# Attention ahead of two dense layers on one core: U of two heads on the two column halves of TensorE, row sums by a product of their own, scores as fp32 products

## The chip, the cores and the metric

One core of a Trainium2 chip runs the whole program. The metric is the device time of one execution in microseconds (us); of the kernel before there are three timed executions, and their median is the number that counts. One further execution was recorded by the hardware profiler, and every duration below comes from that one. The engines are named PE (TensorE, with PEld for its weight loads), DVE (VectorE), ACT (ScalarE), POOL (GpSimd) and SP (SyncE, which issues the transfers).

## The reference, cut to what matters

Attention over 2 batches of 12 heads, 448 positions, 64 values a head, causal; then a dense layer of 768 to 1024 with a softmax gate and a layer norm, back to 768; then a second dense layer 768 to 2048 to 768. Only the attention is touched by the change.

```python
scores = scale * np.matmul(q, k.transpose(0, 1, 3, 2))
mask = np.triu(np.ones((seq, seq), dtype=bool), k=1)
scores = np.where(mask, -1000000000.0, scores)
scores = scores - np.max(scores, axis=-1, keepdims=True)
attn = np.exp(scores)
attn = attn / (np.sum(attn, axis=-1, keepdims=True) + 1e-09)
return np.matmul(attn, v).astype(np.float32)
...
h = x @ w_in
...
return (ln @ w_out).astype(np.float32)
...
h = np.maximum(x @ w_in, 0.0)
return (h * h @ w_out).astype(np.float32)
```

## The kernel before

The 24 heads are worked as 12 pairs. Of a pair, head 0 lies on SBUF partitions 0 to 63 and head 1 on 64 to 127, so a score product of one head uses one half of the array's rows. Two number formats occur on PE: F32R, a rounded fp32, which the dense layers and the scores use, and plain fp32, which U uses. To keep the scores exact in F32R, k and q are split in a high part (`kq_hi`, op H, L242, on ACT, tile HI) and a low rest (`kq_lo`, op L, L246, on DVE, tile LO), and `scores` (ops Sa and Sb, L317) adds three products: HI·HI, LO·HI and HI·LO.

For each pair, in order: the raw maxima of the scores are taken from HI alone (`max_mm`, ops S0a to S0c, L257, tile mxp; `max_red`, L272, on DVE), turned by PE (mT, L284) and brought to the other layout by a transfer (row, rowd; tile MR). Sa and Sb then compute the scores with the keys on the partitions, in two halves of 512 columns: Sa holds the blocks of 448 and 64 columns, Sb those of 320 and 192 (table `HALF`), and a last product with MR subtracts the maxima (L325; for pair 0 by L333). ACT takes the exponential of a half (ops ea1 and eb1, L349, tile PP, 5 buffers), POOL clears what lies above the diagonal (ka, kb, L346). `pv` (ops Ua and Ub, L358) multiplies by V in plain fp32: the tile VR holds for each head 64 columns of V and 64 columns of ones, so that the product U has the 64 outputs of a head on partitions 0 to 63 and the row sums on 64 to 127, head by head, each in a PSUM bank of its own. ACT copies U to E (L369), and transfers carry the sums to a small tile, their reciprocals to DRAM, and from there as `bc` back over the partitions; POOL multiplies (norm, L399, once for each head), and ACT and DVE split the result in two parts, the tiles xT (L407, L411).

What follows is `h_tile` (L474, products h of the first dense layer), its softmax and norm, `y0` and `y1` (L621), and the second dense layer (L756, products h and o).

The order of all this up to y1 is written out by hand: the string `SEQ` lists operations as name.index, and each engine executes its own in that order. PSUM is four slots of two banks, handed out in the order of SEQ (`bank2`, `give`). SP issues the transfers in the same order. The split weights w of the dense layers are made by DVE, ACT and, in the second layer, POOL.

## Time and profile before

| | us |
|---|---|
| median of 3 executions | 458.17 (457.73 to 458.36) |
| the profiled execution, whole | 457.37 |
| its span from first to last instruction | 455.6 |
| PE busy | 448.8 (99%) |
| DVE, ACT, POOL busy | 274.8, 164.2, 121.8 |

A page of the profile has the busy time of each engine, the span in 40 slices, the chain of work that ended last (followed back from the last instruction to what released each step), and groups of equal instructions. Further views list groups with each tile shape apart, one stretch in order of time, or the busy time of all engines in chosen stretches. A busy share near 100% of one engine together with a chain that lies almost wholly on it means that the sum of that engine's work sets the time. In these views a plain fp32 matmul appears as two records, an F32R one as one; a shape such as 64\*128 ahead of a tile's size is rows times columns of the array that a matmul uses.

### The profile page before, as it was taken

The numbers are of one execution on the slowest core, as the hardware profiler recorded it, in microseconds if no ns is written. First come the engines' busy times: TensorE is split into PE (matmuls) and PEld (weight loads), VectorE is DVE, ScalarE is ACT, GpSimd is POOL, SyncE is SP. The second block draws the span as 40 slices with busy tenths as digits, with TensorE's granted clock in tenths as the row PEclk, the third lists the DMA queues.
The fourth block names the chain that finished last, engine by engine and source line by source line (L and its number), as shares of the span: only waits on it lengthen the run. The fifth ranks groups of instructions, "written<-read, shape, count | busy, mean of one in ns | idle before, by whom it ended". The sixth has DMA issues, their size and how long they took to land.

```text
span 455.6 us, 6327 instructions
## 1 busy us (share of the span) xinstructions
PE 448.8 (99%) x2439; PEld 392.7 (86%) x2439; DVE 274.8 (60%) x524; ACT 164.2 (36%) x211; POOL 121.8 (27%) x122
## 2 busy tenths in 40 slices
PE   8999999999999999999999999999999999999996
PEld 6777777787888899988899999999999999999995
DVE  8889787756669998741347566665763424343221
ACT  3465665523556626231133333424331011210101
POOL 3125546364321011110021322313223131132310
PEclk9999999999999999999999999999999999999999
DMA  8357766232172360000042423424343342733403
GB/s 253 129 156 222 223 169 160 57 93 75 41 293 123 109 238 2 0 1 0 0 139 70 140 84 124 126 83 138 74 134 98 111 135 74 241 104 124 120 19 121
DMA packets 41400, 52.45 MB, mean 115 GB/s; under 512 B 18202, under 2 KB 32026, under 8 KB 40986
## 3 DMA queue, kind: packets, MB, share of 16 engines
q1 hardware_dynamic: 41370, 52.05, 37.1%
q8 instruction: 19, 0.31, 0.3%
q14 instruction: 11, 0.09, 0.1%
HBM read 49.16 MB, written 2.80 MB: 114 GB/s over the span
## 4 chain that ended last, share of the span: by engine, by line
PE 96%; DVE 0%; ACT 0%; issue 0%
PE h L756 25%; PE o L756 25%; PE h L474 13%; PE y L621 13%; PE U L358 10%; PE s L317 5%; PE mxp L257 2%; PE s L325 1%; PE T L599 1%; PE mxp L284 0%; PE s L333 0%; DVE o L790 0%; ACT o L790 0%
## 5 line engine op out<-in xcount | busy, mean ns | idle before, releaser
L756 PE MATMUL h<-yT,w 128*128 128x480 f32 x576 | 115.4, 362 | 0.0
L756 PE MATMUL o<-g,w 128*128 128x480 f32 x576 | 115.4, 362 | 0.0
L756 PEld LDWEIGHTS h<-yT,w 128*128 128x128 f32 x576 | 107.9, 187 | 7.4
L756 PEld LDWEIGHTS o<-g,w 128*128 128x128 f32 x576 | 107.9, 187 | 7.3
L677 POOL TENSOR_TENSOR w<-wf,w 128x768 fp32r<-128x768 f32 x32 | 59.3, 1852 | 203.0 <-ACT w L674 203.0
L674 ACT CAST w<-wf 128x768 fp32r<-128x768 f32 x32 | 26.8, 836 | 134.8 <-DVE wf L151 103.5
L149 DVE TENSOR_SCALAR wf<-raw 128x768 int32<-128x768 int32 (+1 forms) x46 | 26.8, 582 | 79.6 <-DMA raw<-in_moe_w_out_dram 51.7
L474 PE MATMUL h<-w,xT 128*128 128x512 f32 x252 | 59.5, 393 | 0.0
L621 PE MATMUL y<-lnT,w 128*128 128x384 f32 (+1 forms) x288 | 58.5, 363 | 0.0
L621 PEld LDWEIGHTS y<-lnT,w 128*128 128x128 f32 x288 | 51.9, 188 | 5.6
L474 PEld LDWEIGHTS h<-w,xT 128*128 128x128 f32 x252 | 46.8, 188 | 9.6
L358 PE MATMUL U<-PP,VR 128*128 128x448 f32 (+1 forms) x192 | 49.2, 400 | 0.3
L150 DVE SCALAR_TENSOR_TENSOR wf<-raw,wf 128x768 int32<-128x768 int32 (+1 forms) x46 | 47.2, 1027 | 1.6
L151 DVE SCALAR_TENSOR_TENSOR wf<-raw,wf 128x768 int32<-128x768 int32 (+1 forms) x46 | 46.5, 1011 | 1.6
L358 PEld LDWEIGHTS U<-PP,VR 128*128 128x128 f32 x192 | 32.1, 190 | 16.6 <-issue 11.4
L399 POOL TENSOR_TENSOR x<-E,bc 64x448 f32<-64x448 f32 x24 | 32.2, 1341 | 45.9 <-DMA bc<-d 42.9
L272 DVE CUSTOM_DVE_ANT_0 JK<-mxp,MK 112x336 bf16<-112x336 f32 (+2 forms) x96 | 38.8, 445 | 9.4 <-PE mxp L257 8.5
L349 ACT ACTIVATE PP<-s 128x1024 f32<-128x1024 f32 x24 | 24.5, 1023 | 12.9 <-PE s L325 7.2
L738 DVE TENSOR_TENSOR relu<-h,relu 128x896 f32<-128x896 f32 x16 | 17.5, 1092 | 14.6 <-ACT relu L737 14.6
L346 POOL TENSOR_SCALAR_AFFINE_SELECT PP<-PP 128x256 f32<-128x256 f32 (+1 forms) x48 | 20.5, 459 | 20.1 <-ACT PP L349 19.5
L740 ACT CAST g<-relu 128x896 fp32r<-128x896 f32 x16 | 15.1, 942 | 18.6 <-DVE relu L738 18.6
L650 DVE TENSOR_TENSOR yT<-y,yT 128x384 fp32r<-128x384 f32 (+1 forms) x12 | 7.4, 624 | 22.4 <-ACT yT L649 22.4
(75 smaller groups left out, 348.2 us busy)
## 6 DMA issues: line engine op xcount, KB each, us to landing
raw<-in_moe_w_out_dram SPq DMA_DIRECT2D x24, 768.0 KB
raw<-in_moe_w_in_dram SPq DMA_DIRECT2D x16, 768.0 KB
r<-in_kq_dram SPq DMA_DIRECT2D x12, 448.0 KB
VR<-in_v_dram SPq DMA_DIRECT2D x12, 256.0 KB
raw<-in_moe_w_in_dram SPq DMA_DIRECT2D x12, 256.0 KB
raw<-in_moe_w_in_dram SPq DMA_DIRECT2D x3, 1024.0 KB
bc<-d SPq DMA_DIRECT2D x12, 224.0 KB
out_dram<-o SPq DMA_DIRECT2D x6, 240.0 KB
```

The costliest lines, as they stand in the source:

```text
L149: nc.vector.tensor_scalar(xi, hw, 3, 0x3FFFFFFF, ALU.logical_shift_left, ALU.bitwise_and)
L150: nc.vector.scalar_tensor_tensor(xi, hw, -0x40000000, xi, ALU.bitwise_and, ALU.bitwise_or)
L151: nc.vector.scalar_tensor_tensor(xi, lw, 29, xi, ALU.logical_shift_right, ALU.bitwise_or)
L272: nc.vector.tensor_tensor_reduce(JK[t], b[0:JP, h, o : o + nk], MK[:, S - nk :], 1.0, NEG, ALU.add, ALU.max, mx[i][:, 4 * h + t : 4 * h + ...
L349: nc.scalar.activation(PP[n % NPP], sb[n], AF.Exp, scale=0.125)
L358: nc.tensor.matmul(UB[i][:, h, q0:S], VR[i % 3][:, t, h, :], PP[(2 * i + a) % NPP][:, h, o : o + nq], start=t == 0, stop=t == 2,)
L399: nc.gpsimd.tensor_tensor(x[D * h : D * h + D], e[0:D, h], bc[:, h], ALU.mult)
L474: nc.tensor.matmul(b[:, half, :], xT[c][s][:, t * P : t * P + P], W1[c][:, w, 512 * half : 512 * half + 512], start=(c == 0 and s == 0 and ...
L621: nc.tensor.matmul(b[:, ci, 0:n], WO[fi][:, w, c * P : c * P + P], M["lnT"][a][s][:, fi, :], start=(fi == 0 and w == 0 and s == 0), stop=( ...
L674: nc.scalar.copy(W2[n][:, 0], w_f["2", n])
L677: nc.gpsimd.tensor_tensor(W2[n][:, 1], w_f["2", n], f(W2[n][:, 0]), ALU.subtract)
L756: nc.tensor.matmul(flat(b)[:, o : o + n], w[:, wp, c : c + P], ops[s][:, x : x + n], start=first and r == 0, stop=last and r == 2,)
```

## The change

`pv` gives head 0 the columns 0 to 63 of the array and head 1 the columns 64 to 127: V of a head is 64 columns without ones, both heads write one PSUM bank, on different partitions, and the loops are turned so that the heads alternate. The row sums come from two new operations: `row_add` (op ad) adds on POOL the blocks of a pair's two halves that belong to the same query positions, with three additions into a new tile `ps`; `row_sum` (op Us) multiplies PP and `ps` with a tile of ones, again one head on each half of the columns, 448 columns a head. `scores` makes one plain fp32 product straight from k and q in place of the three of F32R; kq_lo, LO and the raw tiles are gone, k and q land in four buffers KQ, and H reads them. `u_out` becomes two ACT instructions, the sums leave by two transfers and `bc` comes back by two, norm is one instruction over both heads. PP has 6 buffers. SEQ is a new order of everything up to y1.

```diff
-KLO_POOL = (0,)
-NPP = 5
+NPP = 6
+NKQ = 4
...
 SEQ = """
-load_r.0 fl.0 fl.1 fl.2 fl.3 H.0 load_r.1 fl.4 L.0 S0b.0 S0c.0 mxb.0 fl.5 S0a.0 fl.6 mxc.0 fl.7 mxa.0 H.1 load_r.2
...
+fl.0 fl.1 fl.2 load_r.0 fl.3 H.0 fl.4 load_r.1 fl.5 H.1 S0c.0 load_r.2 S0a.0 S0b.0 fl.6 fl.7 lq.0 load_r.3 lq.1 mxc.0
...
             def load_r(i):
-
-                kq_raw[i] = t = raw.tile([P, 2, S], F32, tag="r", name="r")
-                nc.sync.dma_start(t, kq[i])
+                nc.sync.dma_start(KQ[i % NKQ][:, :, 0:S], kq[i])
...
             def scores(n):
                 i, a = divmod(n, 2)
-                HIk, HIq, LOk, LOq = (x[i % 3][:, j] for x in (HI, LO) for j in range(2))
+                K, Q = (KQ[i % NKQ][:, j] for j in range(2))
                 s = sb[n] = bank2("s")
-                first = True
-                for K, Q in ((HIk, HIq), (LOk, HIq), (HIk, LOq)):
-                    for t, o, q0, nq in HALF[a]:
-                        for h in range(2):
-                            r = slice(D * h, D * h + D)
-                            nc.tensor.matmul(
-                                s[:, h, o : o + nq], K[r, P * t : P * t + P], Q[r, q0 : q0 + nq], start=first, stop=False
-                            )
-                        first = False
+                for t, o, q0, nq in HALF[a]:
+                    for h in range(2):
+                        r = slice(D * h, D * h + D)
+                        nc.tensor.matmul(
+                            s[:, h, o : o + nq],
+                            K[r, P * t : P * t + P],
+                            Q[r, q0 : q0 + nq],
+                            start=t == HALF[a][0][0],
+                            stop=False,
+                        )
...
-                for h in range(2):
-                    for t, o, q0, nq in HALF[a]:
+                for t, o, q0, nq in HALF[a]:
+                    for h in range(2):
                         nc.tensor.matmul(
-                            UB[i][:, h, q0:S],
+                            UB[i][D * h : D * h + D, 0, q0:S],
                             VR[i % 3][:, t, h, :],
                             PP[(2 * i + a) % NPP][:, h, o : o + nq],
...
+            def row_add(i):
+
+                pa, pb = (PP[(2 * i + a) % NPP] for a in range(2))
+                ps[i] = p = lat.tile([P, 2, Q2], F32, tag="ps", name="ps", bufs=2)
+                nc.gpsimd.tensor_tensor(p, pa[:, :, 512 - Q2 :], pb[:, :, 512 - Q2 :], ALU.add)
+                for o, x in ((P, pb[:, :, 0 : Q2 - P]), (2 * P, pa[:, :, 0 : Q2 - 2 * P])):
+                    nc.gpsimd.tensor_tensor(p[:, :, o:], p[:, :, o:], x, ALU.add)
+
+            def row_sum(i):
+
+                p, pa = ps.pop(i), PP[(2 * i) % NPP]
+                for o, x in ((0, pa[:, :, D : D + P]), (P, p)):
+                    n = x.shape[2]
+                    for h in range(2):
+                        nc.tensor.matmul(
+                            UB[i][D * h : D * h + D, 1, o : o + n], ONES, x[:, h], start=o == 0, stop=o > 0
+                        )
...
-                nc.scalar.activation(ee[i], U[:, :, 0:S], AF.Identity, bias=SE)
+                nc.scalar.activation(ee[i][0 : D + 1, 1], U[0 : D + 1, 1, 0:S], AF.Identity, bias=SE[0 : D + 1])
+                nc.scalar.copy(ee[i][:, 0], U[:, 0, 0:S])
...
-                for h in range(2):
-                    nc.gpsimd.tensor_tensor(x[D * h : D * h + D], e[0:D, h], bc[:, h], ALU.mult)
+                nc.gpsimd.tensor_tensor(x, e[:, 0], bc, ALU.mult)
```

Three places show what this does to the engines' own orders. On PE, the scores of one half of a pair in the middle of the attention, before (HI, LO and MR are the tiles named above, NEG the constant that the maxima are multiplied with; a number behind a name is the buffer):

```order
L317 MATMUL s<-HI_118 128x448 x2
L317 MATMUL s<-HI_118 128x64 x2
L317 MATMUL s<-HI_118,LO_121 128x448 x2
L317 MATMUL s<-HI_118,LO_121 128x64 x2
L317 MATMUL s<-LO_121,HI_118 128x448 x2
L317 MATMUL s<-LO_121,HI_118 128x64 x2
L325 MATMUL s<-MR_124,NEG_127 128x512 x2
```

and of a whole pair with the change:

```order
L308 MATMUL s<-KQ_119 128x320 x2
L308 MATMUL s<-KQ_119 128x192 x2
L319 MATMUL s<-MR_124,NEG_125 128x320 x2
L319 MATMUL s<-MR_124,NEG_125 128x192 x2
L308 MATMUL s<-KQ_119 128x448 x2
L308 MATMUL s<-KQ_119 128x64 x2
L319 MATMUL s<-MR_124,NEG_125 128x512 x2
```

Twelve F32R matmuls of a half have become four of fp32, and the two heads still alternate. On PE, U of one pair, before:

```order
L358 MATMUL U<-PP_140,VR_136 128x448
L358 MATMUL U<-PP_140,VR_136 128x64
L358 MATMUL U<-PP_140,VR_136 128x448
L358 MATMUL U<-PP_140,VR_136 128x64
L257 MATMUL mxp<-HI_119 128x224 x2
L257 MATMUL mxp<-HI_120 128x448 x2
L257 MATMUL mxp<-HI_119 128x448 x2
L358 MATMUL U<-PP_141,VR_136 128x320
L358 MATMUL U<-PP_141,VR_136 128x192
L358 MATMUL U<-PP_141,VR_136 128x320
L358 MATMUL U<-PP_141,VR_136 128x192
```

and with the change (64x448 is 64 output columns by 448):

```order
L352 MATMUL U<-PP_139,VR_134 64x448 x2
L352 MATMUL U<-PP_139,VR_134 64x64 x2
L250 MATMUL mxp<-HI_117 128x336 x2
L250 MATMUL mxp<-HI_117 128x112 x2
L352 MATMUL U<-PP_140,VR_134 64x320 x2
L352 MATMUL U<-PP_140,VR_134 64x192 x2
L250 MATMUL mxp<-HI_117 128x224 x2
L250 MATMUL mxp<-HI_115 128x448 x2
L374 MATMUL U<-PP_139,ONES 64x128 x2
L374 MATMUL U<-ps,ONES 64x320 x2
```

The heads alternate instead of following one another, and a third block, the row sums, stands behind other work. On POOL, some rows of the same stage, before:

```order
L346 AFFINE_SELECT PP_140<-PP_140 128x2x64
L346 AFFINE_SELECT PP_140<-PP_140 128x2x128
L399 TENSOR_TENSOR x<-E,bc 64x448 x2
L346 AFFINE_SELECT PP_141<-PP_141 128x2x128 x2
L346 AFFINE_SELECT PP_138<-PP_138 128x2x128 x2
```

and with the change:

```order
L416 TENSOR_TENSOR x<-E,bc 128x448
L340 AFFINE_SELECT PP_140<-PP_140 128x2x128 x2
L340 AFFINE_SELECT PP_139<-PP_139 128x2x64
L340 AFFINE_SELECT PP_139<-PP_139 128x2x128
L364 TENSOR_TENSOR ps<-PP_139,PP_140 128x640
L366 TENSOR_TENSOR ps<-ps,PP_140 128x2x192
L366 TENSOR_TENSOR ps<-ps,PP_139 128x2x64
```

The two norm instructions are one, and the three additions stand right behind the causal fills that they read.

## Rows read from the trace of the kernel before

**Rows 1.** The page: span, busy time of each engine, granted clock in 40 slices.

```profile
span 455.6 us, 6327 instructions
...
PE 448.8 (99%) x2439; PEld 392.7 (86%) x2439; DVE 274.8 (60%) x524; ACT 164.2 (36%) x211; POOL 121.8 (27%) x122
...
PEclk9999999999999999999999999999999999999999
```

**Rows 2.** The chain that ended last, shares of the span by line.

```profile
by line: PE h L756 25.3%; PE o L756 25.3%; PE h L474 12.7%; PE y L621 12.6%; PE U L358 10.4%; PE s L317 4.7%; PE mxp L257 1.9%; PE s L325 1.4%; PE T L599 1.3%; PE mxp L284 0.4%; PE s L333 0.3%; DVE o L790 0.1%; ACT o L790 0.1%; issue 0.1%
```

**Rows 3.** The same chain from 47 to 57 us: start us, us, what.

```profile
47.88 0.76 PE s L317 x12
48.63 0.26 PE s L325 x4
48.90 0.89 PE s L317 x12
49.79 0.32 PE s L325 x2
...
51.50 2.09 PE U L358 x8
...
54.25 1.92 PE U L358 x8
```

**Rows 4.** PE groups, shapes apart: records | busy us, mean ns | idle before.

```profile
L358 PE MATMUL U<-PP,VR 128*128 128x448 f32 x48 | 23.5, 571 | 0.3
...
L317 PE MATMUL s<-HI 64*128 64x320 f32 x24 | 4.5, 369 | 0.0
```

**Rows 5.** PE weight loads in order of time: start us, us, what, records [idle before].

```profile
51.43 0.30 PEld L358 LDWEIGHTS U<-PP,VR 128*128 128x128 f32 x2
51.91 0.19 PEld L358 LDWEIGHTS U<-PP,VR 128*128 128x128 f32 x1 [0.19 <-issue]
52.29 0.41 PEld L358 LDWEIGHTS U<-PP,VR 128*128 128x128 f32 x3 [0.19 <-issue]
...
53.26 0.19 PEld L358 LDWEIGHTS U<-PP,VR 128*128 128x128 f32 x1 [0.19 <-issue]
53.52 0.46 PEld L257 LDWEIGHTS mxp<-HI 64*128 64x128 f32 x6
```

**Rows 6.** Busy time of the engines in two stretches of the attention.

```profile
core 0: us, PE busy (x) PEld busy (x) DVE busy (x) ACT busy (x) POOL busy (x), PEclk, DMA share, GB/s
15.00:55.00 40.00, 39.81 (x313) 29.64 (x313) 33.84 (x112) 23.99 (x32) 15.97 (x26) 1.00 0.67 196
55.00:92.00 37.00, 36.93 (x267) 26.93 (x266) 29.27 (x82) 22.34 (x29) 18.42 (x27) 1.00 0.48 134
```

**Rows 7.** POOL, ACT and DVE groups that the change touches, shapes apart.

```profile
L399 POOL TENSOR_TENSOR x<-E,bc 64x448 f32<-64x448 f32 x24 | 32.2, 1341 | 45.9 <-DMA bc<-d 42.9 <-DVE xT L411 2.2
L346 POOL TENSOR_SCALAR_AFFINE_SELECT PP<-PP 128x256 f32<-128x256 f32 x36 | 16.2, 471 | 8.9 <-ACT PP L349 8.6
L246 POOL TENSOR_TENSOR LO<-r,HI 128x896 fp32r<-128x896 f32 x1 | 2.1, 2094 | 2.5 <-ACT HI L242 2.5
L369 ACT ACTIVATE E<-U,SE 128x896 f32<-128x896 f32 x12 | 12.1, 1010 | 17.6 <-PE U L358 12.3 <-issue 2.5 <-PE mxp L284 2.1
L407 ACT CAST xT<-x 128x448 fp32r<-128x448 f32 x12 | 6.8, 563 | 16.1 <-POOL x L399 16.0
L246 DVE TENSOR_TENSOR LO<-r,HI 128x896 fp32r<-128x896 f32 x11 | 13.0, 1180 | 0.5 <-ACT HI L242 0.5
```

**Rows 8.** ACT and DVE groups that copy y out of PSUM.

```profile
L649 ACT CAST yT<-y 128x512 fp32r<-128x512 f32 x6 | 3.5, 587 | 23.9 <-PE y L621 21.7 <-DVE yT L650 2.3
...
L650 DVE TENSOR_TENSOR yT<-y,yT 128x512 fp32r<-128x512 f32 x6 | 4.2, 692 | 20.3 <-ACT yT L649 20.3
...
L650 DVE TENSOR_TENSOR yT<-y,yT 128x384 fp32r<-128x384 f32 x6 | 3.2, 555 | 2.1 <-ACT yT L649 2.1
```

**Rows 9.** The chain again, where the y products begin.

```profile
160.44 15.60 PE y L621 x90
```

More of the change, by code (lines that the diff above doesn't have):

```diff
@@ new lines @@
+lq.4 mxb.0 S0b.1 load_v.0 S0a.1 fl.8 mxa.0 mxb.1 mxa.1 lq.2 mxr.0 Sa.0 H.2 ea1.0 S0c.1 mxc.1 S0a.2 S0b.2 mT.1 row.1
+H.3 Sb.0 mxa.2 mxb.2 rowd.1 ka.0 eb1.0 S0c.2 mxc.2 S0b.3 Sb.1 load_r.4 mT.2 mxb.3 Ua.0 lq.5 eb1.1 kb.0 S0c.3 lq.3 ad.0
+row.2 S0a.3 mxc.3 H.4 mxa.3 rowd.2 Sa.1 Ub.0 mT.3 ea1.1 Us.0 S0b.4 row.3 load_v.1 lq.6 wf.0 Sb.2 E.0 eb1.2 mxb.4 Sa.2
+load_r.5 kb.1 ea1.2 rowd.3 S0a.4 ka.1 Sa.3 S0c.4 Sb.3 H.5 load_v.2 mxa.4 mxc.4 sums.0 S0a.5 ad.1 mT.4 load_r.6 lq.8
+ea1.3 eb1.3 recips.0 mxa.5 row.4 Ua.1 S0b.5 ka.2 H.6 wh.0 Ub.1 S0c.5 lq.7 kb.2 mxb.5 rcd.0 S0a.6 mxc.5 load_v.3 rowd.4
@@ new lines @@
+Us.1 Sa.4 ad.2 load_r.7 kb.3 mxa.6 mT.5 E.1 row.5 S0b.6 ea1.4 Ua.2 Sb.4 H.7 mxb.6 S0c.6 spread.0 ka.3 sums.1 eb1.4
+ad.3 mxc.6 S0a.7 Ub.2 mT.6 S0b.7 norm.0 kb.4 ld.3 row.6 ka.4 recips.1 mxa.7 x_hi.0 Us.2 rowd.5 E.2 Ua.3 Ub.3 x_lo.0
+rcd.1 load_r.8 mxb.7 S0c.7 Sb.5 eb1.5 Sa.5 ad.4 H.8 mxc.7 rowd.6 mT.7 kb.5 Sb.6 ea1.5 wl.0 sums.2 row.7 Us.3 spread.1
+recips.2 S0a.8 eb1.6 load_v.4 norm.1 Sa.6 rcd.2 load_r.9 rowd.7 x_hi.1 kb.6 Ua.4 ea1.6 Ub.4 E.3 ka.5 wf.1 S0b.8
+spread.2 x_lo.1 Us.4 ka.6 mxa.8 load_r.10 sums.3 norm.2 H.9 S0c.8 ad.5 Sb.7 mxb.8 S0a.9 E.4 mxc.8 Sa.7 recips.3
@@ new lines @@
+load_v.5 eb1.7 mxa.9 S0b.9 x_hi.2 mT.8 Ua.5 ea1.7 S0c.9 ad.6 H.10 lq.9 rcd.3 mxb.9 Ub.5 load_v.6 sums.4 mxc.9 x_lo.2
+S0b.10 row.8 Ua.6 mT.9 spread.3 load_r.11 Us.5 ka.7 norm.3 recips.4 row.9 mxb.10 rowd.8 wh.1 S0a.10 Ub.6 E.5 mxa.10
+S0c.10 rcd.4 lq.10 kb.7 x_hi.3 load_g.0 H.11 mxc.10 x_lo.3 Us.6 wl.1 Sb.8 eb1.8 mT.10 Sa.8 ad.7 rowd.9 load_v.7 S0b.11
+spread.4 sums.5 row.10 norm.4 lq.11 ea1.8 recips.5 mxb.11 E.6 Sa.9 Ua.7 load_v.8 rowd.10 S0a.11 Ub.7 kb.8 x_hi.4
+S0c.11 ka.8 ea1.9 Us.7 rcd.5 mxa.11 Sb.9 mxc.11 mT.11 ld.4 row.11 spread.5 Sa.10 sums.6 eb1.9 x_lo.4 Ua.8 wf.2 rowd.11
@@ L183, in attention_moe_kernel @@
             qk_ = ExitStack()
-            raw = qk_.enter_context(pool("raw", bufs=3, side="right"))
             qk = qk_.enter_context(pool("qk", side="right"))
@@ L190, in attention_moe_kernel @@
             HI = [qk.tile([P, 2, 512], F32R, name=f"HI{i}") for i in range(3)]
-            LO = [qk.tile([P, 2, 512], F32R, name=f"LO{i}") for i in range(3)]
+            KQ = [qk.tile([P, 2, 512], F32, name=f"KQ{i}") for i in range(NKQ)]
             MR = [qk.tile([P, D + S], F32R, name=f"MR{i}") for i in range(3)]
@@ L223, in attention_moe_kernel @@
                 nc.vector.memset(f(HI[i][:, :, S:]), 0.0)
-                nc.vector.memset(f(LO[i][:, :, S:]), 0.0)
+            for i in range(NKQ):
+                nc.vector.memset(KQ[i][:, :, S:], 0.0)
             nc.gpsimd.memset(MK, 0.0)
@@ L229, in attention_moe_kernel @@
             nc.gpsimd.tensor_scalar_mul(NID, ident[0:JP, 0:JP], -1.0)
-            for i in range(3):
-                nc.vector.memset(VR[i][:, :, :, D:], 1.0)
+            nc.vector.memset(ONES, 1.0)
             mx = {}
@@ L238, in attention_moe_kernel @@
             rr = {}
+            ps = {}
             xs = {}
             def kq_hi(i):
[L242 to L246 removed]
+                nc.scalar.copy(HI[i % 3][:, :, 0:S], KQ[i % NKQ][:, :, 0:S])
             MAXG = {"a": ((3, 0),), "b": ((2, 0), (0, 336)), "c": ((1, 0),)}
@@ L373, in sums @@
                 c = lat.tile([JP, 8], F32, tag="sc", name="sc", bufs=2)
-                nc.sync.dma_start(c, ee[i][D : D + 1].rearrange("o h s -> o (h s)").rearrange("o (p j) -> o p j", j=8))
+                for h in range(2):
+                    r = ee[i][D * h : D * h + 1, 1].rearrange("o (p j) -> o p j", j=8)
+                    nc.sync.dma_start(c[JP // 2 * h : JP // 2 * h + JP // 2], r)
                 rr[i] = c
@@ L390, in spread @@
                 d = rr.pop(i)
-                bc = lat.tile([D, 2, S], F32, tag="bc", name="bc", bufs=1)
-                nc.sync.dma_start(bc, d.rearrange("(h s) -> h s", h=2).unsqueeze(0).broadcast_to((D, 2, S)))
+                bc = lat.tile([P, S], F32, tag="bc", name="bc", bufs=1)
+                for h in range(2):
+                    nc.sync.dma_start(
+                        bc[D * h : D * h + D], d[S * h : S * h + S].unsqueeze(0).broadcast_to((D, S))
+                    )
                 rr[i] = bc
```

59 lines of the change are left out of this document (21 added, 38 removed).

## The prediction

> **What bounds the kernel now.** I read the page first: PE is busy 448.8 of 455.6 us at the full granted clock, 2.4 GHz, and no other engine passes 60% [rows 1]. The chain of waits says the same with more weight: its links are PE nearly without exception, 10.4% of the span in U, 4.7% in the score products, and waits do not show [rows 2]. In the two attention stretches PE is busy 39.81 of 40 and 36.93 of 37 us, while DVE reaches 33.84, and POOL 18.42 [rows 6]. So a microsecond of PE work saved or added in the attention is a microsecond of the whole, as long as no other engine becomes late. Work of DVE, ACT and POOL that goes or comes is worth nothing by itself.
>
> **What PE's work costs here.** A half of one pair's scores takes 0.76 us (320 and 192 columns) or 0.89 us (448 and 64) [rows 3]. Three products of 512 columns for two heads, one column a cycle at 2.4 GHz, are 3 x 1024 / 2.4 = 1.28 us if the heads follow one another and 0.64 if they run side by side. The rows lie below 1.28, so two matmuls on different halves of the array's rows do run together; the form rows say it again: 24 score records of 369 ns mean are 8.9 us, packed in 4.5 busy us, while 48 records of U at 571 ns, 27.4 us, fill 23.5 [rows 4]. U is plain fp32. Each matmul is two records (48 for 24), and within U the fourth weight load starts 0.38 us behind the third, while 448 columns stream: two cycles a column (448 x 2 / 2.4 = 373 ns) and record, four a matmul [rows 5]. Ua and Ub have 1024 columns of matmul each, 1024 x 4 / 2.4 = 1.71 us. Ub's 1.92 [rows 3] is that plus 0.21: the first load and the emptying of the array around a block (U's last load starts at 53.26, the next user's at 53.52, where loads within a run stand 0.11 apart [rows 5]: 0.15 for the change), and a few ns for each record. Ua's 2.09 has 0.17 more, because a 64-column record (53 ns) is shorter than a load (0.11).
>
> **Part 1, U on two column halves.** If two fp32 matmuls on different columns run together as F32R ones on different rows do, the streams of Ua, Ub and Us (448 columns a head) are 0.853, 0.853 and 0.747 us, 12 x 2.453 = 29.4. Around them: a few ns for each record, 0.03 a block or 1.1 for 36; half of Ua's extra, 0.1 x 12 = 1.2; and 0.15 for each time that the array is given over, which is 30 times, since in the order six of the 36 blocks stand directly behind another: 4.5. Sum 36.2, against 10.4% of 455.6 = 47.4 us: **minus 11.2**. No row shows column halves at work. From above the price is no overlap at all: the same columns take 4.9 us a pair, 12 x 2.453 = 29.4 more; from below, all 30 hand-overs covered by other loads, 4.5 less. I take full overlap, since its nearest row is the row halves.
>
> **Part 2, scores in fp32.** A half is 512 columns side by side at four cycles, 0.853 us, plus 0.03, plus 0.1 for the 64-column records of Sa: 1.87 us a pair against 0.89 + 0.76 = 1.65. That is 12 x 0.22 = **plus 2.6**, for less preparation elsewhere. The subtraction of the maxima (0.26 to 0.32 us a half [rows 3]) and the maxima themselves stay. Bounds: minus 0.5, if the records' overhead vanishes; plus 23 with no overlap of fp32 on row halves.
>
> **Part 3, the new order on PE.** Blocks of U between products of h now change the array's division, where U before had the same one as h. The order shows eight such returns, 0.11 for a load and 0.15 for emptying, of which 0.1 is counted in part 1: **plus 1.0** (0 to 2).
>
> **Part 4, off PE, each at nothing, and its cover.** DVE loses eleven low parts of 1180 ns, POOL one of 2094 [rows 7]. ACT copies U in two instructions; a copy of 448 columns takes 563 ns, so about 1.2 us for 1.01 [rows 7], 2 us more in a stage where it works 60% of the time [rows 6]. POOL gets the most: 448 elements cost it 1341 ns in norm and 896 cost 2094 in the low part [rows 7], 2.3 to 3.0 ns each, so 640 + 384 + 128 elements are 2.7 to 3.4 us a pair, and norm gives back half of its 2.7. With four fills of some 0.46 and norm at 1.2, POOL works about 6.1 us for a pair. PE needed 18.8% of 455.6 us (U, s, mxp with L284, L325 [rows 2]) for twelve, 7.1 a pair, and needs 6.4 after parts 1 and 2. It is covered, narrowly: other blocks stand between a pair's fills and Us in PE's order (in the rows shown, two of maxima between Ub and Us). What is queued behind them on POOL are the next pair's fills, and behind those Ua; and a pair's PSUM slot is held until Us and E are through. If the additions took over about 4.2 us, PE would wait. SP's loads of k and q now wait for the scores of four pairs earlier, not for H and L of three; the row transfers (rowd) stand behind them on that queue. By the order the load of pair i + 4 stands behind Sb of pair i, so it waits for work that is already done. The third load of the second layer's weights (l2.2) and the last copy of y (yo.2) move to the end: PE reaches what yo.2 writes after 4 x 6 matmuls of 0.2 us (25.3% for 576 [rows 2]), 4.8 us into the second layer, and these weights 14 us in; yp.2 and yo.2 together need 0.59 of ACT and 2 x (0.69 + 0.56) of DVE, 3.1 us [rows 8]. Both are covered; uncovered they would cost 1 to 2 us once.
>
> **The sum.** Minus 11.2 plus 2.6 plus 1.0 is minus 7.6. The profiled execution is 457.4 us whole, 1.8 more than its span; it becomes 449.8. It lies 0.8 under the median of the three, so a median would be 450.6; I say 450.
>
> **The rivals.** *In turn, not side by side.* A matmul of fp32 is two records. Head 0's two stand ahead of head 1's two in the queue, and both of head 0's need the same half of the array. If PE starts records strictly in order, head 1 begins only when head 0's second record has begun, and a block of four matmuls has its first and last records alone. Its time is then head 0's first record, its second with head 1's first, head 1's second with head 0's short ones, and head 1's short ones: Sa and Ua 3 x 0.38 + 0.16 = 1.30 us instead of 0.98, Sb and Ub 3 x 0.274 + 2 x 0.167 = 1.16 instead of 0.88, Us (two of 128 columns, three of 320) 1.03 instead of 0.78. That is 0.60 a pair for the scores, 0.60 for U, 0.25 for Us: 12 x 1.45 = 17.4 us, so 457.4 - 7.6 + 17.4 = **467**, slower. For it: the two records per matmul, and no row in which a record overtakes a waiting one. Against it: the rows of the 320-column pairs show both heads in flight, and nothing in this trace has two records for one half ahead of the other's, so it is not tested. It decides once less than half of the records overlap: at 44% of these 17.4 us the gain is gone. The Trainium skill's "TensorE: Matmul & The Clock Gate", in "The mechanism" of its part 3, states that matmuls start and end in program order, with loads alone pulled ahead; by that rule the result would be this rival's.
>
> The Trainium skill's "TensorEngine Tiling (Array Packing)", under "Key Properties", says that tiles work in parallel and that a change of division empties the array. The trace agrees with the first for row halves and with the second by its 0.15 us; no row shows either for columns.
>
> *fp32 does not overlap on one or both kinds of half.* Rows alone: 450 + 20 = 470; columns alone: 480; neither: about 500. Speaks for it: no row has fp32 on half an array. Against it: a record with two cycles a column asks for less data in a cycle than F32R does.
>
> *POOL becomes the bound.* At 5 us of additions a pair, 0.4 to 0.5 us late for each pair: 5 us back, **455**. For it: 6.1 of 6.4 us. Against it: the rates of 896 elements.
>
> **How the numbers follow.** Side by side 0.60; POOL late 0.07; in order 0.24; no overlap of fp32 on a kind of half 0.07; a mixture that ends within 0.2% (about what a measurement of this kernel can tell from no change) 0.02. Faster by more than that: 0.60 + 0.07 less 0.01 = 0.66. Same: 0.03. Slower: 0.31. Both signs are likely, so the likeliest case's own range stands apart: 445 (hand-overs covered and records free, 4.5 + 0.5 less) to 454. The range that holds 8 in 10 must reach to the in-order case: 445 to 468.
>
> **What would show it.** After the change a half of the scores should stand in the chain with 0.85 to 1.0 us, Ua and Ub with 1.0 to 1.2, Us with 0.8 to 1.0; the records of a fp32 shape should have about twice the busy time in their summed durations. 1.2 to 1.3 for each block with starts one record apart is the in-order rival; 1.8 and more is no overlap. Idle PE ended by ps or PP of POOL is the third. PE should reach the first y product at 153 instead of 160.4 us [rows 9] if all holds. Wrong it would be, above all, through the one thing that no row shows: how PE takes two-record matmuls on halves.

## The result, and the profile after

| | before | after |
|---|---|---|
| median of 4 executions each | 458.26 (457.73 to 458.73) | 453.54 (452.57 to 454.35) |
| ratio | | 0.990, 95% interval 0.987 to 0.992 |
| the profiled execution, whole | 457.37 | 452.57 |
| its span | 455.6 | 450.7 |

The change makes the kernel 1% faster. The forecast was 450: the sign holds, and so does the mechanism on PE, but of the 8.2 us forecast 4.7 came. 3.5 us are missing, 2.8 of them also in the profiled execution (449.8 forecast, 452.57 measured). The page of the kernel after, in the lines that answer to [rows 1], and POOL's 40 slices besides:

```profile
span 450.7 us, 6365 instructions
...
PE 440.6 (98%) x2439; PEld 372.7 (83%) x2439; DVE 265.2 (59%) x511; ACT 163.8 (36%) x223; POOL 151.5 (34%) x145
...
POOL 1599888894310011110113131322213132132310
PEclk9999999999999999999999999999999999999999
```

PE's work fell by 8.2 us, from 448.8 to 440.6; the sum of the prediction said 7.6. The span fell by 4.9. Span less busy time, PE's waiting, went from 6.8 to 10.1 us: 3.3 us of the gain went into waits. POOL, busy for some four tenths of the attention before [rows 6], is busy for eight or nine tenths of most of it. PE's waits from 5 us up to the start of the y products show the rest (columns: engine, line, what ended the wait: us in total, times, longest). Before:

```profile
PE fill L503 <- DVE mx L272: 0.5, 1, 0.5
PE mxp L284 <- DVE mx L272: 0.4, 1, 0.4
```

and after:

```profile
PE s L308 <- ACT E L382: 1.3, 1, 1.3
PE h L492 <- DVE lnT L631: 1.0, 1, 1.0
PE T L617 <- ACT h L588: 0.6, 1, 0.6
PE mxp L250 <- DVE mx L265: 0.6, 1, 0.6
PE U L352 <- DMA VR<-in_v_dram: 0.5, 1, 0.5
PE mxp L277 <- DVE mx L265: 0.4, 1, 0.4
```

Two waits of 0.9 us together became six of 4.4. No single row is large and each has another releaser: ACT, DVE, a transfer. That is why the chain, which was PE throughout [rows 2], now wanders: PE 76%, POOL 8%, DMA 6%, DVE 5%. The first y product starts here (start us, us, what), against 160.44 [rows 9] and the 153 that was forecast:

```profile
155.86 15.60 PE y L639 x90
```

The 2.9 us by which it is late are the miss of the profiled execution: from there on both kernels do nearly the same.

**The heads do run side by side.** The forms of PE after, as in [rows 4] (records | busy us, mean ns | idle before):

```profile
L308 PE MATMUL s<-KQ 64*128 64x448 f32 x48 | 11.6, 562 | 1.4 <-ACT E L382 1.3
L352 PE MATMUL U<-PP,VR 128*64 128x448 f32 x48 | 11.6, 562 | 0.5 <-DMA VR<-in_v_dram 0.5
```

48 records of 562 ns are 27.0 us, and they fill 11.6 busy us: a factor of 2.3, on row halves (64\*128) and column halves (128\*64) alike. U's 48 records of 571 ns filled 23.5 us before, a factor of 1.2 [rows 4]. The chain where nothing waits, as in [rows 3]:

```profile
70.25 1.01 PE U L352 x8
...
71.56 0.91 PE U L374 x8
72.47 1.06 PE s L308 x8
...
73.96 1.12 PE s L308 x8
...
75.37 1.88 PE U L352 x16
```

A block of U takes 1.01 where it took 2.09 or 1.92 [rows 3]; Ua and Ub without work between them take 1.88 together; Us costs 0.91. A half of the scores takes 1.06 or 1.12 (0.94 at another place), where it took 0.76 or 0.89 in [rows 3]; only the 0.94 lies within the 0.85 to 1.0 that were forecast.

The lines of PE give the parts of the sum. U's records cover 49.2 us before and 25.1 + 11.7 (Us) after, 12.4 less; the scores 24.9 and 26.9; the products h of the first dense layer 59.5 and 61.3. The granted clock is 1.00 throughout in both traces.

**POOL.** Its groups after, to be held against [rows 7]:

```profile
L340 POOL TENSOR_SCALAR_AFFINE_SELECT PP<-PP 128x256 f32<-128x256 f32 x36 | 23.1, 659 | 3.1 <-ACT PP L343 3.1
L364 POOL TENSOR_TENSOR ps<-PP,PP 128x640 f32<-128x640 f32 x12 | 19.6, 1635 | 0.2
L416 POOL TENSOR_TENSOR x<-E,bc 128x448 f32<-128x448 f32 x12 | 15.9, 1326 | 20.0 <-DMA bc<-d 16.3 <-PE s L319 1.9 <-DVE mx L265 1.8
L366 POOL TENSOR_TENSOR ps<-ps,PP 128x384 f32<-128x384 f32 x12 | 13.2, 1101 | 0.9
L366 POOL TENSOR_TENSOR ps<-ps,PP 128x128 f32<-128x128 f32 x12 | 9.0, 751 | 0.9
```

The additions cost 1.64 + 1.10 + 0.75 = 3.49 us a pair, a little over the 2.7 to 3.4 of the prediction; the fills, untouched by the change, went from 471 to 659 ns. In the two attention stretches POOL and DVE stand like this, to be held against [rows 6]:

```profile
15.00:55.00 40.00, 38.69 (x339) 24.13 (x340) 31.29 (x120) 27.29 (x40) 35.85 (x46) 1.00 0.64 196
55.00:92.00 37.00, 35.89 (x264) 21.54 (x264) 31.21 (x68) 21.30 (x32) 31.91 (x34) 1.00 0.52 162
```

POOL works 67.8 of 77 us, twice as much as before, and PE, full before, leaves 2.4.

### The profile page after: what moved, and what is told of

Read it like the earlier page. It is cut to its first block, busy times and chain, and to the rows that moved or that the text cites. A ratio compares the mean times of both kernels' runs of the same rounds, so it can differ in the third digit from the quotient of the medians.

```text
span 450.7 us, 6365 instructions
## 1 busy us (share of the span) xinstructions
PE 440.6 (98%) x2439; PEld 372.7 (83%) x2439; DVE 265.2 (59%) x511; ACT 163.8 (36%) x223; POOL 151.5 (34%) x145
## 4 chain that ended last, share of the span: by engine, by line
PE 76%; POOL 8%; DMA 6%; DVE 5%; SPq 2%; ACT 1%; issue 1%; POOLq 0%; DVEq 0%
PE h L774 26%; PE o L774 26%; PE y L639 13%; PE h L492 5%; DMA bc<-d 3%; POOL PP L340 2%; POOL ps L364 2%; POOL ps L366 2%; POOL x L416 2%; PE s L308 2%; PE fill L521 1%; PE U L352 1%; DMA sc<-E 1%; DMA raw<-in_moe_w_out_dram 1%; SPq L408 1%
## 5 line engine op out<-in xcount | busy, mean ns | idle before, releaser
L150 DVE TENSOR_SCALAR wf<-raw 128x768 int32<-128x768 int32 (+1 forms) x46 | 28.5, 620 | 81.5 <-DMA raw<-in_moe_w_out_dram 57.3
L492 PE MATMUL h<-w,xT 128*128 128x512 f32 x252 | 61.3, 396 | 1.0 <-DVE lnT L631 1.0
L152 DVE SCALAR_TENSOR_TENSOR wf<-raw,wf 128x768 int32<-128x768 int32 (+1 forms) x46 | 47.3, 1027 | 1.6
L151 DVE SCALAR_TENSOR_TENSOR wf<-raw,wf 128x768 int32<-128x768 int32 (+1 forms) x46 | 46.7, 1015 | 1.6
L265 DVE CUSTOM_DVE_ANT_0 JK<-mxp,MK 112x336 bf16<-112x336 f32 (+2 forms) x96 | 39.1, 445 | 10.8 <-PE mxp L250 9.9
L340 POOL TENSOR_SCALAR_AFFINE_SELECT PP<-PP 128x256 f32<-128x256 f32 (+1 forms) x48 | 28.5, 625 | 13.7 <-ACT PP L343 13.7
L308 PE MATMUL s<-KQ 64*128 64x448 f32 (+3 forms) x192 | 26.9, 398 | 1.4 <-ACT E L382 1.3
L308 PEld LDWEIGHTS s<-KQ 64*128 64x128 f32 x192 | 16.6, 186 | 11.3 <-issue 5.4
L352 PE MATMUL U<-PP,VR 128*64 128x448 f32 (+3 forms) x192 | 25.1, 390 | 0.5 <-DMA VR<-in_v_dram 0.5
L366 POOL TENSOR_TENSOR ps<-ps,PP 128x384 f32<-128x384 f32 (+1 forms) x24 | 22.2, 926 | 1.9
L352 PEld LDWEIGHTS U<-PP,VR 128*64 128x64 f32 x192 | 11.5, 136 | 13.5 <-issue 7.6
```

Of the source, the lines that this page charges most:

```text
L150: nc.vector.tensor_scalar(xi, hw, 3, 0x3FFFFFFF, ALU.logical_shift_left, ALU.bitwise_and)
L151: nc.vector.scalar_tensor_tensor(xi, hw, -0x40000000, xi, ALU.bitwise_and, ALU.bitwise_or)
L152: nc.vector.scalar_tensor_tensor(xi, lw, 29, xi, ALU.logical_shift_right, ALU.bitwise_or)
L265: nc.vector.tensor_tensor_reduce(JK[t], b[0:JP, h, o : o + nk], MK[:, S - nk :], 1.0, NEG, ALU.add, ALU.max, mx[i][:, 4 * h + t : 4 * h + ...
L308: nc.tensor.matmul(s[:, h, o : o + nq], K[r, P * t : P * t + P], Q[r, q0 : q0 + nq], start=t == HALF[a][0][0], stop=False,)
L340: nc.gpsimd.affine_select(ap, ap, [[0, 2], [1, m]], ALU.is_ge, 0.0, base=0, channel_multiplier=-1)
```

## The experiments

Theory to begin with: the halves bring the gain as the prediction worked it out, and what is lost is lost through the buffers and the row sums' round trip, by which a pair's E leads over transfers, reciprocal and normalise to x. Rivals: POOL's sheer load; a part of the records in turn; and the new order itself.

### Was it in turn after all?

In `heads_turn` the loops of `pv` are put back, so that all four records of head 0 stand ahead of those of head 1:

```diff
-                for t, o, q0, nq in HALF[a]:
-                    for h in range(2):
+                for h in range(2):
+                    for t, o, q0, nq in HALF[a]:
```

> The changed kernel with the two loops of pv exchanged, so that all matmuls of head 0 in a block stand ahead of those of head 1; same work. If PE keeps a queue for each half of the array, or looks many records ahead: no change, blocks of 1.0 and 0.9 us, 453.5. If a record can pass only the one or two that wait directly ahead of it: head 1 begins when head 0's last record has begun, Ua and Ub take about 1.8 us each, 12 x 1.6 = 19 us slower, 472. If records start strictly in order, as in the rival of the prediction, the same 472, but then the changed kernel could not have had 1.0.

Measured: 453.50 (453.12 to 454.24), ratio to before 0.990 (0.987 to 0.992), the same as the changed kernel. The timeline of PE in a window of 0.04 us at the start of a U block in `heads_turn` (start us, us, what; an entry spans its records):

```profile
75.27 0.60 PE L352 MATMUL U<-PP,VR 128*64 128x448 f32 x2
```

Two 448-column records start within these 40 ns, and the next two 0.4 us later. The trace doesn't name the column half, but two of one half would stand 0.4 us apart; so the second is head 1's, although in the program three more records of head 0 stand between them. The forms agree, 48 records of 563 ns in 11.7 us:

```profile
L352 PE MATMUL U<-PP,VR 128*64 128x448 f32 x48 | 11.7, 563 | 0.0
```

So a record for one half of the array passes records that wait for the other half, three of them at least. The rival in order falls, with either arrangement of the loops. The rule of the Trainium skill's "TensorE: Matmul & The Clock Gate", "The mechanism" of part 3, that matmuls start in program order, does not describe this trace; the measurement decides.

### What the halves of U are worth

`undo_U` keeps the new order and the fp32 scores, and gives U, sums, E and norm their form of before:

```diff
-                            UB[i][D * h : D * h + D, 0, q0:S],
+                            UB[i][:, h, q0:S],
...
-            VR = [per.tile([P, 4, 2, D], F32, name=f"VR{i}") for i in range(3)]
-            ONES = per.tile([P, D], F32, name="ONES")
+            VR = [per.tile([P, 4, 2, 2 * D], F32, name=f"VR{i}") for i in range(3)]
```

> The changed kernel with U and the row sums in the form of before (value columns with ones beside them, one head after the other over all rows of the array; no additions, no product of sums), everything else and the order of the rest as changed. Theory (the halves of U are what the change gained): the TensorE work grows by the 11.2 us that part 1 of the prediction took off, to about 452 us busy; the additions' 3.5 us a pair leave GpSimd, so of the 4.8 us of TensorE gaps one or two go; 461 to 464 us, slower than before, because the fp32 scores and the new order by themselves only cost. Rival (the new order or the scores bring the gain): at or below 458 us.

Measured: 465.89 (464.29 to 466.79), ratio 1.017 (1.015 to 1.019). Its page, with a span of 462.2 us:

```profile
PE 451.2 (98%) x2343; PEld 388.6 (84%) x2343; DVE 263.8 (57%) x514; ACT 162.9 (35%) x211; POOL 122.3 (26%) x121
```

This is longer than the 461 to 464 expected. PE's busy time is 10.6 us above that of the changed kernel: this is part 1, forecast at 11.2, together with part 3's changes of the array's division, which count the other way and which this U does not need. Against the kernel before it is 2.4 us up: the fp32 scores and the new order. Its span is 6.6 us longer than before, so the other 4.2 are waiting, with POOL no busier than before; one wait alone is 2.5 us,

```profile
PE s L308 <- ACT E L381: 2.5, 1, 2.5
```

so PE waits in the new order also without the additions. That wait ends at 61 us, and then the granted clock falls (columns as in [rows 6]; PEclk is the third from the end):

```profile
60.00:64.00 4.00, 3.02 (x17) 2.01 (x18) 2.34 (x12) 3.73 (x5) 0.28 (x2) 0.78 0.52 135
64.00:68.00 4.00, 4.00 (x15) 2.58 (x15) 1.51 (x9) 0.55 (x2) 0.37 (x2) 0.79 0.66 173
```

These shares are those of some 3.4 us at 0.50, 1.2 instead of 2.4 GHz. An estimate from them: 1.7 us of this kernel's PE busy time come from the clock, so that at the full clock the two differences would be about 8.9 and 0.7. The rival that order or scores bring the gain falls.

### Undoing the scores

`undo_scores` puts the three F32R products back into the new order, with `kq_lo` (L) directly behind H and three buffers of HI and LO:

> The changed kernel with the scores as three F32R products again, and their low part on DVE right behind H in the new order; U and the row sums stay as changed. By part 2 of the prediction PE has 2.6 us less to do. Theory (PE's sum alone): 451. Theory (DVE, busy 31 of 40 us, gets 12 x 1.18 us more and holds up POOL further while its instructions with two inputs run): the maxima and the fills come later, PE idles 3 to 6 us more, 454 to 458.

It took 480.05 (479.07 to 480.60). Three buffers are too few here: the new order writes the HI of pair i + 3 ahead of the scores of pair i, so these used other pairs' parts. It was repeated with four buffers:

```diff
-            HI = [qk.tile([P, 2, 512], F32R, name=f"HI{i}") for i in range(3)]
+            HI = [qk.tile([P, 2, 512], F32R, name=f"HI{i}") for i in range(4)]
+            LO = [qk.tile([P, 2, 512], F32R, name=f"LO{i}") for i in range(4)]
```

> The changed kernel with the scores' three products of rounded parts, as before, with four buffers of the rounded and of the remaining parts, and the subtraction on VectorE; U and order as changed. Theory (the prediction's part 2, price on TensorE alone): TensorE's work falls by 2.6 us and the time to about 451 us. Rival (the fp32 scores pay on VectorE): in this order VectorE has 62.5 us of work between 15 and 92 us without the subtractions; 12 of them at 1.18 us bring 14.2 us, 76.7 of 77 us, and every one has two inputs and so holds GpSimd too. Then TensorE waits for maxima and fills, with gaps of 10 us and more in sum: 463 us or more.

Measured: 475.93 (475.56 to 477.55), ratio 1.040 (1.038 to 1.042). The largest of PE's waits, and DVE's own between 5 and 95 us:

```profile
PE mxp L257 <- DVE mx L272: 9.3, 6, 2.5
PE mxp L284 <- DVE mx L272: 5.1, 5, 2.6
```

```profile
DVE LO L245 <- ACT HI L242: 14.9, 9, 5.0
```

PE waits for maxima, as the rival said, but not because DVE has no time left: DVE stands 14.9 us at the subtraction, waiting for ACT's HI, and the maxima queue behind it. That is where I put L in an order that was not made for it. So the run shows what a misplaced wait on DVE costs, and does not price the scores by themselves. The cost is in two parts: PE waits 13.3 us longer than in the changed kernel (23.4 against 10.1), and it is also busy 9.9 us longer (450.5 against 440.6), although the products themselves should save 2.6: its granted clock is 0.80 from 15 to 55 us and 0.94 from 55 to 92. What the fp32 scores cost on PE is read from the lines before and after instead, 1.9 us.

### Where the 3.3 us go: buffers, POOL, DVE

ACT in the changed kernel waits for POOL ahead of E (L381), since E has two buffers and E of pair i needs norm of pair i - 2 to be done:

```profile
ACT E L381 <- POOL x L416: 20.5, 7, 7.5
```

`e3` gives E a third buffer:

```diff
-                ee[i] = lat.tile([P, 2, S], F32, tag="E", name="E", bufs=2)
+                ee[i] = lat.tile([P, 2, S], F32, tag="E", name="E", bufs=3)
```

> The changed kernel with three buffers of E in place of two, nothing else. Theory 1 (the part of the gain that is missing was lost because E of a pair waits for norm of two pairs earlier, which waits for its sums to come back over four transfers): ACT's 20.5 us of waits for POOL ahead of E shrink, PE's idle 1.3 us near 54 us goes, 1 to 2 us faster than the changed kernel, 451.5 to 452.5 as a median. Theory 2 (POOL's throughput alone is late, the buffers of E only hand that on): the same 453.5 within 0.5 us.

Measured: 450.48 (450.01 to 453.29), ratio 0.985 (0.980 to 0.989), better than the 451.5 to 452.5 of the theory. Three of the four executions took 450.01 to 450.91, and one, at 453.29, lies in the range of the changed kernel. The wait of s for E is gone; of the others the largest are

```profile
PE U L352 <- DVE mx L265: 1.3, 1, 1.3
PE mxp L250 <- DVE mx L265: 0.7, 1, 0.7
```

`one_add` leaves out the second and third addition (L366), and with them those blocks of the row sums:

```diff
-                for o, x in ((P, pb[:, :, 0 : Q2 - P]), (2 * P, pa[:, :, 0 : Q2 - 2 * P])):
-                    nc.gpsimd.tensor_tensor(p[:, :, o:], p[:, :, o:], x, ALU.add)
```

> The changed kernel with the second and third addition of row_add left out, so the row sums lack those blocks; POOL has 1.85 us less to do for each pair, 22 us in all. Theory 2 (POOL late): PE's idle time falls from 4.8 us to under 3, POOL leaves the chain between 16 and 50 us, 2 to 3.5 us faster than the changed kernel, 450 to 451.5. Theory 1 (the wait for E's buffer): under 1 us faster, since norm still waits for its transfers.

Measured: 451.32 (450.06 to 452.35), ratio 0.985 (0.981 to 0.988). POOL works 47.5 of the 77 us instead of 67.8:

```profile
15.00:55.00 40.00, 38.49 (x336) 24.13 (x337) 29.90 (x116) 27.27 (x40) 26.83 (x36) 1.00 0.63 195
55.00:92.00 37.00, 34.92 (x263) 21.35 (x260) 27.84 (x69) 21.35 (x32) 20.68 (x26) 1.00 0.52 160
```

and PE is no fuller for it in these stretches. Three tenths of POOL's work taken away bring 2.2 us by the medians, but loosely: two of the four executions took 450.06 and 450.36, two 452.27 and 452.35, and in the profiled one, of 452.27, PE waits for 10.0 us, as long as in the changed kernel. The waits at 54 and 57 us stay. POOL as the bound, the third rival, explains no more than a part. `e3_third` asks the same the other way round, with three buffers of E and the third addition done by PE instead:

```diff
-                for o, x in ((0, pa[:, :, D : D + P]), (P, p)):
+                for o, x in ((0, pa[:, :, D : D + P]), (P, p), (3 * P, pa[:, :, 0:D])):
```

> The changed kernel with three buffers of E and the third addition of each pair replaced by a product of 64 columns on TensorE. Theory (GpSimd's 0.75 us a pair are worth more than TensorE's 0.11 us a pair and half, some 1.5 us in all): TensorE's work up by 1.4 us, gaps down by at most 1 us: 450.5 to 451.5 us, no better than three buffers of E alone, since the gaps there come from VectorE. Rival (GpSimd decides): gaps fall by 2 us and more, 449.5 us or less.

Measured: 452.77 (451.06 to 452.83), ratio 0.987 (0.985 to 0.989), by the medians slower than `e3`, and somewhat more than the theory's 451.5. The largest of PE's waits is now 2.5 us ahead of U at 58 us, and the view names POOL's addition as what ended it. The trace's semaphore events say otherwise: PE's queue passed the mark of DVE's maxima at 57.85, 0.02 us after it was set, and U began its weight loads 0.19 us later, as it did in `e3` behind the same mark, where no addition ended in between. DVE had stood 2.9 us at the reciprocal for the sums' transfer. So this is the gap of `e3` at 55 us again, and longer; the share of POOL's load is not what is short.

**Why POOL's fills grew.** In the timeline of the changed kernel POOL and DVE stand together thus (start us, us, engine, line, what):

```profile
43.66 2.21 POOL L340 TENSOR_SCALAR_AFFINE_SELECT PP<-PP 128x256 f32<-128x256 f32 x2
44.30 1.30 DVE L151 SCALAR_TENSOR_TENSOR wf<-raw,wf 128x1024 int32<-128x1024 int32 x1
45.63 1.31 DVE L152 SCALAR_TENSOR_TENSOR wf<-raw,wf 128x1024 int32<-128x1024 int32 x1
45.84 2.11 POOL L416 TENSOR_TENSOR x<-E,bc 128x448 f32<-128x448 f32 x1
```

Two fills that take 0.41 each when undisturbed take 2.21 here, and norm, 1.14 undisturbed, 2.11: the second fill and norm each began while DVE was at an instruction that reads two tiles. Of the 36 fills of 256 columns, seven lasted 1.38 to 1.42 us, every one begun beside such an instruction (L151, L152 or L487); 24 lasted 0.40 to 0.41. The five between, of 0.78 to 0.87 us, began beside a shorter instruction of two tiles (L428, three) or beside L150 (two; the first of the two fills above is one), which reads a single tile. All twelve ended 0.26 to 0.27 us after the DVE instruction beside which they began, so that they lost little less than what was left of it. The fifteen that began beside the maxima (L265), which read one operand from PSUM, took 0.40 to 0.41. Before, three fills of the 36 were slow. The Trainium skill's "SBUF — State Buffer", "Who interferes with whom", states that a VectorE instruction with two inputs in SBUF contends with a GpSimd instruction that reads SBUF, and that the ports which the two share are an exclusive lock; the trace agrees, with about 1.0 us for a fill beside L151 or L152, and shows a fill held in the same way beside L150. `one_input` makes L151 and L152 read one tile, so that the weights lack the bits which the second would bring; the two instructions also get shorter, 0.78 us where they took 1.30:

```diff
-            nc.vector.scalar_tensor_tensor(xi, hw, -0x40000000, xi, ALU.bitwise_and, ALU.bitwise_or)
-            nc.vector.scalar_tensor_tensor(xi, lw, 29, xi, ALU.logical_shift_right, ALU.bitwise_or)
+            nc.vector.tensor_scalar(xi, hw, -0x40000000, 0, ALU.bitwise_and, ALU.bitwise_or)
+            nc.vector.tensor_scalar(xi, lw, 29, 0, ALU.logical_shift_right, ALU.bitwise_or)
```

> The changed kernel with the two instructions of each weight row's conversion on VectorE that read two tiles (L151 and L152) made to read one, so that the weights come out without those bits; same count, shapes and place. They are also shorter on VectorE. Theory (GpSimd is held while VectorE reads two tiles of SBUF): the mean of the 128x256 fills falls from 659 ns towards the 410 ns of undisturbed ones, no fill that meets L151 or L152 takes over 1 us, and the time falls by 0.5 to 2 us. Rival (the slow fills come from something else, as the memory's share or the semaphores): the fills keep their 650 ns.

Measured: 450.32 (449.77 to 450.65), ratio 0.984 (0.982 to 0.985), more than expected.

```profile
L340 POOL TENSOR_SCALAR_AFFINE_SELECT PP<-PP 128x256 f32<-128x256 f32 x36 | 19.9, 571 | 3.9 <-ACT PP L343 3.9
```

The only two fills left above 1 us stand beside L487, which still reads two tiles; none beside L151 or L152 does. But POOL is not free beside them. The stretch of the timeline above is now

```profile
43.66 1.67 POOL L340 TENSOR_SCALAR_AFFINE_SELECT PP<-PP 128x256 f32<-128x256 f32 x2
44.29 0.78 DVE L151 TENSOR_SCALAR wf<-raw 128x1024 int32<-128x1024 int32 x1
```

and the second fill still ends 0.26 us after L151. Fills of 0.78 to 0.89 us became more, nine instead of five, and seven of the nine began beside L150, L151 or L152, each reading one tile; so the mean fell by 88 ns only. The theory's condition, two tiles, is not what decides: a fill is held for as long as the instruction beside it lasts, and these became shorter. DVE as a whole is busy 39 us less than in the changed kernel (226.4 against 265.2). What share of the 3.2 us comes from shorter holds of POOL and what from DVE's own time this run does not tell apart.

### The round trip

`e3xb2` adds second buffers of x and bc to the third of E (bc by the same edit as x):

```diff
-                x = lat.tile([P, S], F32, tag="x", name="x", bufs=1)
+                x = lat.tile([P, S], F32, tag="x", name="x", bufs=2)
```

> The changed kernel with three buffers of E, two of x and two of bc, nothing else. Theory (the second row of waits is normalise's: it waits for x to be read by VectorE's x_lo and holds the additions behind it on GpSimd): against three buffers of E alone (450.5 us, TensorE gaps 3.7 us) the gap of 1.3 us ahead of U at 55 us goes; 449 to 450 us. Rival (GpSimd is late by its own work and by VectorE's two-input instructions, not by x): as with three buffers of E alone, 450.5 us, with normalise no longer waiting but U at 55 us still late.

Measured: 451.41 (450.91 to 451.91), ratio 0.986 (0.984 to 0.987): no better than E alone. The gap at 55 us, 1.6 us now, is still ended by the maxima, and its chain says why:

```profile
50.81 2.78 DMA sc<-E
...
53.62 0.20 DVE sr L395
53.82 0.49 DVE JK L265
...
55.44 1.09 PE U L352 x8
```

DVE stands at the reciprocal until the sums' transfer has landed; the maxima behind it in its order are late, and with them the PSUM bank that they hold. `e3_late` therefore puts the reciprocals of pairs 2 and 3 one group of maxima later, with the steps that follow them, in the order of `e3xb2`:

```diff
-x_lo.0 rcd.1 load_r.8 mxb.7
+rcd.1 load_r.8 mxb.7 x_lo.0
...
-recips.2 S0a.8
...
-mxa.8 load_r.10 sums.3 norm.2 H.9 S0c.8 ad.5
+mxa.8 recips.2 rcd.2 load_r.10 spread.2 sums.3 H.9 S0c.8 ad.5 norm.2
...
-recips.3 load_v.5 eb1.7 mxa.9
+load_v.5 eb1.7 mxa.9 recips.3
```

> The changed kernel with three buffers of E, two of x and of bc, and five steps of the row sums' round trip put later in the order: the reciprocals of pairs 2 and 3 one group of maxima later on VectorE (with pair 2's transfers behind them), x_lo of pair 0 behind two groups of maxima, normalise of pair 2 behind the additions. TensorE's order is unchanged. Theory (what is left of TensorE's gaps is VectorE standing at a reciprocal for its transfer while maxima queue behind it): the gaps of 1.6 us at 55 us and of 1.5 us at 70 us go, TensorE idles 2 to 2.5 us in all and the time is 448.5 to 450 us, below the 450.5 and 451.4 us with the buffers alone. Rival (it is VectorE's and GpSimd's work, not the place of the steps): the same gaps turn up elsewhere, 450.5 us or more.

Measured: 455.29 (453.89 to 457.43), ratio 0.993 (0.991 to 0.996): by the medians slower than the changed kernel. The theory's sign was right for the two gaps, which are gone, and wrong for the time. One new wait of 4.3 us has taken their place, and SP's queue has one of 3.9:

```profile
PE U L352 <- DMA VR<-in_v_dram: 4.3, 1, 4.3
```

```profile
SPq L401 <- DVE sr L395: 4.8, 2, 3.9
```

V of pair 5 stands on SP behind the sums' transfers, and those waited for the later reciprocal. And the wait costs twice. The windows of `e3_late` from 54 us (columns as in `undo_U` above):

```profile
54.00:58.00 4.00, 0.10 (x1) 0.00 (x0) 1.00 (x6) 0.07 (x1) 1.23 (x2) 0.85 0.65 168
58.00:62.00 4.00, 3.62 (x16) 1.78 (x18) 1.48 (x9) 2.38 (x4) 3.46 (x5) 0.50 0.43 134
62.00:66.00 4.00, 4.00 (x23) 1.95 (x21) 1.70 (x10) 0.32 (x2) 1.86 (x3) 0.50 0.73 189
```

PE stood still from 54.1 to 58.4 us; then its granted clock is 0.50 for these 8 us, and blocks of U take 1.90 us instead of 1.02. That is another 4 us: PE is busy 443.7 us here and 439.4 in `e3xb2`, with the same instructions.

`e3_late_v` puts the loads of V for pairs 5 and 6 ahead of the sums' transfers in `e3_late`, and `e3_v` does that in `e3` without the late steps:

```diff
-load_v.4
+load_v.4 load_v.5
...
-Ub.4
+Ub.4 load_v.6
```

> The kernel before this one (E, x and bc with more buffers, late reciprocals) with the loads of V for pairs 5 and 6 put ahead of the row sums' transfers on SyncE's queue: pair 5's directly behind pair 4's. Theory (the one gap of 4.3 us at 58 us came from the load of V for pair 5, which stood on SyncE behind the sums' transfers that the late reciprocal held): the gap goes, nothing takes its place, TensorE stays at full clock and idles 1 to 2 us; 449 to 450.5 us. Rival (it is conserved work of the other engines, and any order gives some gap): 452 us or more.

> The changed kernel with three buffers of E and the loads of V for pairs 5 and 6 early, reciprocals where the change has them. Theory: the gaps of e3 (1.3 us at 55 us and 0.7 us at 69 us, ended by VectorE's maxima behind a reciprocal) stay, the runs that took 453 us instead of 450 us with three buffers of E do not come back, since they are those in which V was late; 450.0 to 450.6 us in every run. Rival (V's load is not late there): spread as with three buffers of E, 450.0 to 453.3 us.

Measured: `e3_late_v` 454.69 (453.37 to 455.61), ratio 0.992 (0.990 to 0.994); `e3_v` 451.04 (449.43 to 455.66), ratio 0.983 (0.981 to 0.986). Both theories were wrong on the time. In `e3_late_v` the wait for V is gone and a wait of the same length stands at another place, with a chain behind it that can be read engine by engine (PE, ACT, POOL):

```profile
PE mxp L250 <- ACT PP L343: 4.4, 2, 4.2
```

```profile
ACT xT L424 <- POOL x L416: 6.3, 2, 4.4
```

```profile
POOL x L416 <- DMA bc<-d: 3.2, 1, 3.2
```

POOL stands at normalise for the transfer of bc, ACT at x_hi for normalise, the exponentials queue behind x_hi, and PE's slot behind them. In `e3_v` the spread did not narrow: it holds the fastest execution of all kernels here, 449.43, and one of 455.66. The latter is the profiled one, and no load of V stands among PE's waits in it: they are 3.5 us for maxima in two waits and 2.5 us ahead of U, again with DVE at the reciprocal, 2.6 us. So a late V is not why some executions are slow; that stays open.

So what is shown is this: the round trip of the sums touches DVE (reciprocal), SP (three transfers), POOL (normalise) and ACT (E, x_hi), and on each of them something that PE needs stands behind it. Where its steps are moved, the wait appears on another engine. What is not shown is one order that takes all of them away.

## Why the prediction was right, and where it was off

- **Part 1**, minus 11.2: U's lines went down by 12.4 us. Full overlap on column halves, taken from row halves, was right, and the saving was put a little too low; the blocks' lengths fell within the forecast's 1.0 to 1.2 for Ua and 0.8 to 1.0 for Us. `undo_U`, which takes back the changes of division as well and runs in part at half the clock, gives 10.6 less, or about 8.9 by the estimate above.
- **Part 2**, plus 2.6: the scores' lines went up by 1.9. The two rows taken for before, 1.65 us a pair, were on the low side: 4.7% of 455.6 us [rows 2] is 1.78 a pair. Its lower bound is also a slip, since without the overhead 1.71 against 1.65 would be plus 0.7 and not minus 0.5.
- **Part 3**, plus 1.0 (eight times 0.16 is 1.3): the lines of h went up by 1.8, and by 1.5 in `undo_U`, whose U does not change the division. So the new order costs there, but how much of it is the division was not separated.
- Together minus 8.2 was measured where minus 7.6 was forecast. The sum is closer than its parts, since their errors partly cancel.
- **The rivals.** In turn (467) is refuted by the records and by `heads_turn`; no overlap of fp32 (470 and more) by the factor of 2.3. I gave the first of these 0.24, chiefly because no row of before had tested it; that was fair by the rows that there were.
- **Part 4 is the step that failed, in size.** It set everything off PE at nothing and called POOL covered, narrowly. The additions' own 3.49 us a pair stayed below the 4.2 at which I said that PE would wait, and yet PE waits 3.3 us longer. The sum itself came out too low: with fills of 2.4 us a pair instead of 1.8 and norm of 1.33 instead of 1.2, POOL's work for a pair is 7.2 us and not 6.1, more than the 6.4 that PE was to need. And three things were not in it. I held POOL's average for a pair against PE's, but the stage is a chain of handovers, and E's two buffers tie ACT to POOL's normalise: a third buffer gives 3.1 us back, with the same work on POOL. I took POOL's durations from a kernel in which three of 36 fills were held by DVE's instructions; with twice as much POOL work it is twelve. And I looked at who is queued behind the additions, but not at who is queued behind the round trip's waits on DVE, SP and ACT, which a faster PE reaches sooner.
- The rival *POOL becomes the bound*, given 0.07, came nearer in price (455) than the forecast and had part of the right cause: less POOL work (`one_add`) gives back 2.2 us by the medians, and changes that leave POOL's work as it is give as much or more. Its sign, idle PE ended by ps or PP of POOL, did not show in the changed kernel: the releasers named are ACT, DVE and a transfer, behind which POOL acts.
- 453.54 lies within the likeliest case's own range, 445 to 454, by 0.5 us; its upper end had been given no working, so that much is luck.

The fastest arrangement that computes the same is `e3`, the changed kernel with a third buffer of E: 450.48, ratio to before 0.985 (0.980 to 0.989), with `e3_v` beside it within the spread. Its interval overlaps that of the changed kernel (0.987 to 0.992), so the size of this step is less sure than its direction.

## What to carry to other kernels

Work of PE can be summed from its records: here the sum of what a change saves was forecast to within a microsecond. What the saving turns into is decided by the order of the other engines, so for each step with a transfer in it, list what stands behind its wait on its engine and how soon a faster PE will want that. When an engine off the path gets twice the work, look at which instructions of its neighbours it will meet, and at the buffers that tie it to others, and not only at its mean load. A buffer more at such a tie is the first thing to try (one more of E brought some 3 us here, more of x and bc beside it nothing); moving a late step back in the order shifted its wait to the next queue.
